# Four alternating attention layers as one list-scheduled pipeline of 128-token tiles, with block-diagonal scores

## The chip, the cores and the metric

The kernel runs on one core of one Trainium2 chip. The metric is the device time of one execution in microseconds (us), as the median over several runs. Engines are named as the profile does: PE is TensorE (matmul), PEld its weight loads, DVE is VectorE, ACT is ScalarE, POOL is GpSimd, SP the engine that issues the transfers. PSUM is the memory in which this kernel's matmuls leave their results, used here as eight banks; an eviction is the copy of a result out of it by ScalarE or VectorE. The clock in the tables is the share of its full clock that TensorE was granted, as the profile records it. A row group is a strip of 32 of TensorE's rows; in these kernels small matmuls are placed on different row groups so that they run side by side.

## The reference

One sequence of 2048 tokens, 512 features, 32 heads of 16. Four residual layers alternate: A is linear attention over the whole sequence, B is softmax attention over a sliding window of 256 keys. All in bfloat16.

```python
def _A_ref(x, wqkv, wo):                 # ... q, k, v: 32 heads of 16
    phi = lambda t: jnp.where(t > 0, t + 1, jnp.exp(t)) + 1e-6
    pq, pk = phi(q), phi(k)
    kv = jnp.einsum("bhsd,bhse->bhde", pk, v)
    z = jnp.einsum("bhsd->bhd", pk)
    num = jnp.einsum("bhqd,bhde->bhqe", pq, kv)
    den = jnp.einsum("bhqd,bhd->bhq", pq, z)[..., None] + 1e-6
    o = num / den
    # ... heads together
    return o @ wo
def _B_ref(x, wqkv, wo):                 # W = 256
    scores = jnp.einsum("bhqd,bhkd->bhqk", q, k) * (Dh ** -0.5)
    mask = (idx[:, None] - idx[None, :] >= 0) & (idx[:, None] - idx[None, :] < W)
    p = _softmax(jnp.where(mask[None, None], scores, -1e9), axis=-1)
    # ... p @ v, heads together
    return o @ wo
x = x + _A_ref(_layernorm(x), A_wqkv, A_wo)
x = x + _B_ref(_layernorm(x), B_wqkv, B_wo)
x = x + _A_ref(_layernorm(x), A_wqkv, A_wo)
x = x + _B_ref(_layernorm(x), B_wqkv, B_wo)
```

A needs the sum over all tokens (kv, z) before any of its outputs: a true barrier. B needs for a query only the 256 keys up to it.

## The kernel before

Each layer is a few phases, and every engine ends one phase before the next begins. B's attention phase goes pair of heads by pair of heads through a ring of three PSUM score buffers:

```python
def emit_scores(pe, pg):                      # two heads, 128 keys, up to 384 queries
    sl = pg % NSLOT                           # NSLOT = 3
    if pg >= NSLOT:
        pe.wait_ge(s_exp.h, s_exp.v(pg - NSLOT + 1))
    # ...
    for e in range(2):                        # two row groups of TensorE at once
        mm = pe.matmul(ST[sl][:, e, 0:n], lhsT, rhs, start=True, stop=True,
                       tile_position=(32 * (hs % 4), 0))
    s_st.inc(mm)
# TensorE's order
for pg in range(npairs):
    if pg + LA < npairs:                      # LA = 2
        emit_scores(pe, pg + LA)
    emit_pv(pe, pg)                           # waits for the masks of pg; 6 matmuls of 17 columns
# ScalarE
a.activation(self.PTs[:, j % NJS, hp[0] : hp[0] + 2, 0:n], ST[sl][:, :, 0:n],
             ACT.Exp, bias=self.zero1[:], scale=DH ** -0.5)
# VectorE: two triangular masks for each of the two heads
for e in range(2):
    op = v.tensor_tensor(self.PTs[:, js, hs, 0:P], self.PTs[:, js, hs, 0:P], self.maskHi[:], ALU.mult)
    if j + 2 < T:
        op = v.tensor_tensor(self.PTs[:, js, hs, 2 * P : 3 * P],
                             self.PTs[:, js, hs, 2 * P : 3 * P], self.maskLo[:], ALU.mult)
```

The softmax here doesn't subtract the row's maximum and nothing guards it: scores larger than these inputs give would overflow.

## Time and profile before

Median 845 us (843.5 to 846.3).

| stretch, us | what | TensorE | VectorE | ScalarE | clock |
|---|---|---|---|---|---|
| 193 to 402 | attention of the first B | 84% | 80% | 96% | 0.50 |
| 607 to 818 | attention of the second B | 84% | 79% | 95% | 0.50 |

The lines of the page for the whole span: totals of busy time, busy tenths in 40 slices with the granted TensorE clock, and the costliest groups of instructions (line, engine, operation, tiles, shapes and count, then busy us and mean ns of one, then idle time before it and what ended it).

```profile
span 840.9 us, 16707 instructions
PE 666.5 (79%) x5794; PEld 330.4 (39%) x5824; DVE 596.2 (71%) x2784; ACT 614.4 (73%) x856; POOL 6.5 (1%) x24
...
PE   0779685897888888888857877589888888888878
...
DVE  6669695437878778788767776943488787787865
ACT  1668234458999999999557763345599999999983
...
PEclk9989797996555555555779998979955555555559
...
L894 ACT ACTIVATE PTs<-st,zero_15 128x768 bf16<-128x768 f32 (+2 forms) x512 | 404.7, 860 | 21.7 <-PE st L849 10.3
L931 DVE TENSOR_TENSOR PTs<-PTs,maskHi 128x128 bf16<-128x128 bf16 x1024 | 219.5, 220 | 78.9 <-ACT PTs L894 78.1
L868 PE MATMUL U<-vB,PTs 128*128 128x17 bf16 x2880 | 163.0, 179 | 67.5 <-DVE PTs L935 62.9
L849 PE MATMUL st<-qT,kT 16*128 16x384 bf16 (+2 forms) x512 | 121.3, 472 | 2.2 <-PEq L320 2.2
```

Half of the span is B's attention: the long runs of 9 in ScalarE's row, over 5 in the clock's row. There TensorE and VectorE are some 80% busy, and TensorE's clock is half.

### The profile page before, as it was taken

To read this page: it belongs to the slowest core of one execution; us is meant where nothing else is said; L and a number is where in the kernel's file an instruction comes from. 1 tells how busy PE (TensorE), PEld (TensorE's weight loads), DVE (VectorE), ACT (ScalarE), POOL (GpSimd) and SP (SyncE) were. 2 spreads that over 40 slices of the span, in tenths; PEclk is the share of its full clock that TensorE was granted. 3 is DMA by queue.
4 is the path that set the end of the run, shared out by engine and by line. 5 is a ranking of instruction groups with operands and counts; after the bars stand their busy time and mean duration, and the time that the engine had idled before them with its cause. 6 is when DMAs were issued, how large, how long until landed. Compare 5 with 4: busy or idle time off the path is not lost. (4 is left out here: it accounts for less than half of the span.)

```text
span 840.9 us, 16707 instructions
## 1 busy us (share of the span) xinstructions
PE 666.5 (79%) x5794; PEld 330.4 (39%) x5824; DVE 596.2 (71%) x2784; ACT 614.4 (73%) x856; POOL 6.5 (1%) x24
## 2 busy tenths in 40 slices
PE   0779685897888888888857877589888888888878
PEld 0333542343343334433533344344333434334344
DVE  6669695437878778788767776943488787787865
ACT  1668234458999999999557763345599999999983
POOL 1000000000000000000000000000000000000000
PEclk9989797996555555555779998979955555555559
DMA  8000000000000000000000000000000000000003
GB/s 299 0 1 1 1 1 1 1 1 1 1 2 2 2 2 1 2 1 2 1 1 0 1 1 1 1 1 1 1 1 2 2 2 2 2 1 2 1 2 101
DMA packets 5971, 9.46 MB, mean 11 GB/s; under 512 B 384, under 2 KB 4992, under 8 KB 5888
## 3 DMA queue, kind: packets, MB, share of 16 engines
q1 hardware_dynamic: 5472, 6.29, 2.2%
q0 software_dynamic: 416, 2.10, 0.7%
q8 instruction: 47, 0.77, 0.4%
q14 instruction: 36, 0.29, 0.1%
HBM read 6.29 MB, written 2.10 MB: 10 GB/s over the span
## 5 line engine op out<-in xcount | busy, mean ns | idle before, releaser
L894 ACT ACTIVATE PTs<-st,zero_15 128x768 bf16<-128x768 f32 (+2 forms) x512 | 404.7, 860 | 21.7 <-PE st L849 10.3
L931 DVE TENSOR_TENSOR PTs<-PTs,maskHi 128x128 bf16<-128x128 bf16 x1024 | 219.5, 220 | 78.9 <-ACT PTs L894 78.1
L868 PE MATMUL U<-vB,PTs 128*128 128x17 bf16 x2880 | 163.0, 179 | 67.5 <-DVE PTs L935 62.9
L868 PEld LDWEIGHTS U<-vB,PTs 128*128 128x128 bf16 x2880 | 116.1, 106 | 244.5 <-DVE PTs L935 228.5
L935 DVE TENSOR_TENSOR PTs<-PTs,maskLo 128x128 bf16<-128x128 bf16 x896 | 194.8, 217 | 0.0
L849 PE MATMUL st<-qT,kT 16*128 16x384 bf16 (+2 forms) x512 | 121.3, 472 | 2.2 <-PEq L320 2.2
L849 PE MATMUL st<-qT,kTB 32*128 32x384 bf16 (+2 forms) x512 | 122.4, 473 | 0.0
L338 PE MATMUL pst<-ident,xn 128*128 128x128 bf16 x256 | 30.6, 276 | 71.2 <-DVE xn L436 66.4
L376 PE MATMUL pss<-xnT,wB_qk 128*128 128x512 bf16 x248 | 61.9, 390 | 0.6 <-issue 0.2
L376 PE MATMUL pss<-wA_qkv,xnT 128*128 128x512 bf16 x255 | 61.3, 383 | 0.1
L398 ACT ACTIVATE xnT<-pst 128x512 bf16<-128x512 bf16 x64 | 34.8, 595 | 31.7 <-PE pst L338 31.4
L470 DVE TENSOR_SCALAR kTB<-kT,maskB 128x512 bf16<-128x512 bf16 x32 | 11.3, 353 | 64.7 <-ACT kT L417 64.7
L251 ACT ACTIVATE tmpE<-pss,zero_15 128x512 f32<-128x512 f32 x64 | 44.1, 689 | 15.9 <-PE pss L376 8.0
L338 PEld LDWEIGHTS pst<-ident,xn 128*128 128x128 bf16 x256 | 20.2, 119 | 84.2 <-DVE xn L436 51.0
L671 ACT ACTIVATE oTtA<-pstA 128x512 bf16<-128x512 bf16 x32 | 19.1, 597 | 36.2 <-PE pstA L549 36.2
L911 DVE TENSOR_TENSOR o_tok<-U,densb 128x128 bf16<-128x128 f32 x128 | 37.3, 292 | 9.9 <-issue 0.4
L252 ACT ACTIVATE tmpR<-pss,zero_15 128x512 bf16<-128x512 f32 x64 | 44.0, 688 | 0.0
L255 DVE TENSOR_SCALAR tmpE<-tmpE 128x512 f32<-128x512 f32 x64 | 26.9, 420 | 23.7 <-ACT tmpR L252 23.7
L417 ACT ACTIVATE qT<-pss 128x512 bf16<-128x512 f32 x32 | 19.1, 597 | 32.7 <-PE pss L376 32.7
L436 DVE TENSOR_SCALAR xn<-xres,ln_mv,ln_rstd 128x512 bf16<-128x512 bf16 x64 | 26.1, 431 | 18.1 <-PE pst L338 7.3
L376 PEld LDWEIGHTS pss<-wA_qkv,xnT 128*128 128x128 bf16 x256 | 25.5, 100 | 32.5 <-issue 3.9
L376 PEld LDWEIGHTS pss<-xnT,wB_qk 128*128 128x128 bf16 x256 | 25.5, 101 | 30.4 <-issue 2.8
(84 smaller groups left out, 647.5 us busy)
## 6 DMA issues: line engine op xcount, KB each, us to landing
xres<-in_A_x_dram SPq DMA_DIRECT2D x4, 512.0 KB, 5.4
out_dram<-xres SPq DMA_DIRECT2D x16, 128.0 KB, 1.7
wA_qkv<-in_A_wqkv_dram SPq DMA_DIRECT2D x1, 1536.0 KB, 10.2
wB_nat<-in_B_wqkv_dram POOLq DMA_DIRECT2D x1, 1536.0 KB, 9.1
wA_o<-in_A_wo_dram SPq DMA_DIRECT2D x1, 512.0 KB, 11.8
wB_o<-in_B_wo_dram POOLq DMA_DIRECT2D x1, 512.0 KB, 9.6
```

Source lines behind the costliest of these rows:

```text
L251: a.activation(self.tmpE[:, js, :], ps_ap, ACT.Exp, bias=z)
L252: return a.activation(self.tmpR[:, js, :], ps_ap, ACT.Relu, bias=z)
L255: v.tensor_scalar(self.tmpE[:, js, :], self.tmpE[:, js, :], 1.0, 1e-6, op0=ALU.min, op1=ALU.add)
L338: mm = pe.transpose(pst[sl2][:, kt, :], self.xn[:, sl2, kt * P : (kt + 1) * P], self.ident[:])
L376: mm = pe.matmul(pss[:, sl, :], lhsT, rhs, start=(kt == 0), stop=(kt == 3))
L398: s_cp.inc(a.activation(self.xnT[:, :, t * P : (t + 1) * P], pst[sl2][:], ACT.Copy))
L849: mm = pe.matmul(ST[sl][:, e, 0:n], lhsT, rhs, start=True, stop=True, tile_position=(32 * (hs % 4), 0))
L868: mm = pe.matmul(ut[:, hs, 0:17], lhsT, rhs, start=(ci == 0), stop=(ci == len(cl) - 1))
L894: a.activation(self.PTs[:, j % NJS, hp[0] : hp[0] + 2, 0:n], ST[sl][:, :, 0:n], ACT.Exp, bias=self.zero1[:], scale=DH ** -0.5,)
L911: v.tensor_tensor(self.o_tok[:, jd, fd * P : (fd + 1) * P].rearrange("p (h d) -> p h d", d=DH), ut[:, :, 0:DH], dsb.to_broadcast([P, 8, DH ...
L931: op = v.tensor_tensor(self.PTs[:, js, hs, 0:P], self.PTs[:, js, hs, 0:P], self.maskHi[:], ALU.mult)
L935: op = v.tensor_tensor(self.PTs[:, js, hs, 2 * P : 3 * P], self.PTs[:, js, hs, 2 * P : 3 * P], self.maskLo[:], ALU.mult,)
```

## The change

The intent: make all layers one stream of 128-token tiles, so that the projections, norms and evictions of one tile run under the exps of another, and cut the work of the attention itself. The whole program is built as a graph of operations with priorities; a list scheduler in the kernel's Python file orders them on each engine, gives out the eight PSUM banks, and may place an eviction on ScalarE or VectorE. The core of the diff (the rest, nearly all of the file, is cut):

```diff
-for li, kind in enumerate(["A", "B", "A", "B"]):      # phase after phase
-    ...
+def build(self):
+    self.setup()
+    self.layer_a_keys(1, 0)      # first A: keys, values, queries of all tiles
+    self.barrier(1)              # kv sums, M = kv @ Wo, denominators
+    self.middle(2)               # tile by tile: A's output, B, the next A's keys and values
+    self.barrier(2)
+    self.middle(3)               # tile by tile: A's output, B, output
 # scores: two heads (block-diagonal keys) by 64 keys, 320 queries, four row groups at once
+for gq in range(4):
+    rows = slice(32 * gq, 32 * gq + 32)
+    m = e.matmul(K.ps(ps[gq])[:, 0:n], K.kB[rows, j % 4, 2 * f + b, :, :],
+                 K.XQ[rows, f, 64 * blk:64 * blk + n], ..., tile_position=(32 * gq, 0))
-    ACT.Exp, bias=self.zero1[:], scale=DH ** -0.5,
+    e.activation(K.pb[...], K.PS[:, b0:b1 + 1:b1 - b0, 0:n], ACT.Exp, bias=0.0, scale=0.25)
 # one mask instruction for four head pairs, both triangles
+    x = K.pb[:, sl, f, :, o:o + 320].rearrange("p g (w c) -> p g w c", c=64)[:, :, 0:5:4, :]
+    return e.tensor_tensor(x, x, K.tri[:]..., ALU.mult)
 # transposes of normalised tiles and of B's output: by the SP queue, most of them
+    return self.on("SP", name, lambda e: e.dma_start_transpose(out(), src()), ...)
 # 1/sqrt(var) on GpSimd, tile by tile, instead of Ln and Exp on ScalarE for all tiles
+    self.on("POOL", "pow", lambda e: e.tensor_tensor(K.rs[:, t, :], K.ve[:, t, :], K.negh[:], ALU.pow), ...)
+PAR = dict(cap_s=6, cap_d=2, ...)   # PSUM banks for scores, and for all else, in the middle phases
```

## The prediction

> **What bounds the kernel now.** It runs in phases; windows over the stages show two limits.
> - The two sliding-attention phases (193 to 402 and 607 to 818 us) take 420 of 841 us. ScalarE is busy 200 of 209 us in each: 256 exps follow each other every 0.84 us (timeline). The granted TensorE clock is 0.50 there. VectorE (166 of 209) masks in 1920 small multiplies of 220 ns, one every 0.135 us: about 259 us in all.
> - The other 421 us (both linear layers, B's projections, output products) are bound by no engine: ScalarE and VectorE are 44 to 73% busy. Each phase drains before the next.
>
> **What the change does.**
> 1. *Exp.* A diagonal block took 384 queries per 128 keys, now 320 per 64 keys of two heads: 344k to about 290k ScalarE columns. The 512 exps stay 512, at 640 columns. Their bias becomes an immediate. The Trainium skill ("ScalarE: Activation LUTs", What ACT_TABLE_LOAD costs) puts a pointer operand at about 93 ns; the trace agrees: a 512-wide exp with pointer bias takes 689 ns, a copy 597. Estimate: 0.84 becomes 0.62 us per exp; 430 becomes about 300 us. The relu (64 x 688 ns) goes too.
> 2. *Masks.* 1920 multiplies become 256 over four head pairs: about 259 to 95 us.
> 3. *TensorE.* Scores: four row tiles at once instead of two. Value products stay 2880, at 34 columns instead of 17. Weight products M = KV.Wo replace num, and half the transposes go to the DMA queue (69).
> 4. *Order.* Three long phases (A keys; A out + B + next A keys; A out + B) instead of eight; projections, norms and evictions run under the exps.
>
> **Engine sums after**, counted from the built instruction order, costed at start-to-start times of the trace: ScalarE 300 (exp) + 32 (phi) + 43 (88 copies) = 375 us. VectorE about 390 us. TensorE at full clock (512 columns: 0.216 us, as in the trace): projections 230, value products 80, scores 33, rest 30, = 373, plus some 590 changes of tiling at an estimated 0.08 us = 47: 420 us. Nearly balanced.
>
> **Time.** A-keys prologue 60; barrier and fill of three tiles 18; 16 tiles of middle phase at 13.5 = 216; barrier 22; 16 tiles at 12.2 = 195; tail 9: 520 us. The tile times allow 15 to 20% over the busiest engine, because the evictions share two PSUM banks and scores six. About 130 us of the gain is exps, the rest overlap.
>
> **Clock.** The skill ("TensorE: Matmul & The Clock Gate", HAM clock gate) has two states, half and full, by activity; the trace shows 0.50 in attention, 1.00 in dense projections. With projections mixed in I expect 0.9.
>
> **What would show it.** Right: exp group near 725 ns each, ScalarE total near 375, mask group below 110 us, clock above 0.85, no engine idle over 15 us except at two barriers; ScalarE busy above 80% in the middle phases. Wrong: clock near 0.5 to 0.7 in the middle phases (PE bound, +60 us or more); long ScalarE waits on TensorE scores (PSUM coupling); waits on DMA transposes, whose cost no line of this trace shows.
>
> **What would make it wrong.** Half clock; fewer stalls in the static order than allowed (470); transposes slow or in the way.
>
> Predicted 518 us, 8 in 10 between 470 and 570; faster 0.98, same 0.01, slower 0.01.

## The result, and the profile after

The changed kernel takes 534.2 us (532.6 to 536.3, 4 runs); it is correct. The ratio to before is 0.632 (95% interval 0.631 to 0.634).

The same parts of the page after the change:

```profile
span 532.9 us, 16311 instructions
PE 445.8 (84%) x7124; PEld 289.6 (54%) x7124; DVE 415.8 (78%) x988; ACT 389.4 (73%) x673; POOL 59.1 (11%) x114
...
PE   0399987888999999999877997888998989787676
...
DVE  4497769788988899999765759899799889777543
ACT  0166762689988889899886343389799889899962
POOL 8860001001000010000000000100000000000000
PEclk9999999989999999999887999899899999999756
...
L624 ACT ACTIVATE pb<-ps 128x640 bf16<-128x640 f32 (+4 forms) x512 | 305.9, 675 | 33.1 <-PE ps L612 30.2
L632 DVE TENSOR_TENSOR pb<-pb,tri 128x512 bf16<-128x512 bf16 x224 | 92.7, 415 | 16.4 <-ACT pb L624 15.0
L612 PE MATMUL ps<-XQ,kB 32*128 32x320 bf16 (+4 forms) x1024 | 80.7, 305 | 26.5 <-ACT pb L624 24.9
L652 PE MATMUL ps<-vB,pb 128*128 128x34 bf16 x2880 | 90.6, 179 | 4.9 <-DVE xres L565 2.0
```

The table of stretches, as the windows view gives it for the phases of the new kernel (start:end, length, then busy us and count of each engine, granted clock, DMA share, GB/s), and one stretch of steady state:

```profile
0.00:22.00 22.00, 0.44 (x4) 0.35 (x4) 7.79 (x31) 1.28 (x1) 18.45 (x44) 1.00 0.88 286
22.00:77.00 55.00, 53.18 (x574) 35.53 (x572) 42.55 (x103) 36.31 (x63) 13.69 (x23) 1.00 0.01 2
77.00:98.70 21.70, 16.07 (x248) 10.95 (x248) 18.18 (x36) 6.90 (x15) 2.19 (x4) 1.00 0.01 2
98.70:297.00 198.30, 179.06 (x2868) 108.67 (x2864) 166.07 (x411) 170.22 (x297) 14.86 (x27) 0.96 0.17 29
297.00:346.00 49.00, 42.05 (x667) 32.87 (x667) 37.59 (x81) 17.82 (x33) 2.91 (x6) 0.97 0.02 4
346.00:525.00 179.00, 151.82 (x2740) 99.84 (x2738) 142.01 (x326) 156.32 (x266) 6.97 (x12) 0.92 0.14 32
...
180.00:230.00 50.00, 47.78 (x785) 29.54 (x784) 46.03 (x112) 45.29 (x76) 4.39 (x8) 1.00 0.17 34
```

In the stretch of steady state TensorE, VectorE and ScalarE are 96, 92 and 91% busy at once. Over the whole first middle phase they are 90, 84 and 86% busy, over the second 85, 79 and 87%. The exps fill these two phases of 198 and 179 us. Around them stand 22 us in which little but GpSimd works, 55 us of the first A's keys, values and queries, 22 us to fill the pipeline after the first barrier, and 49 us at the second barrier, in which ScalarE is busy for 18.

The attention itself became cheaper for TensorE. Two pieces of the timeline (start, length, engine, line, operation and count) show it. The first is from the old order, in the run `before_both` below, where TensorE hardly waits; the second is from the changed kernel:

```profile
301.33 0.50 PE L850 MATMUL st<-qT,kT 16*128 16x384 bf16 x2
301.76 0.33 PE L869 MATMUL U<-vB,PTs 128*128 128x17 bf16 x6
302.02 0.50 PE L850 MATMUL st<-qT,kTB 32*128 32x384 bf16 x2
302.45 0.33 PE L869 MATMUL U<-vB,PTs 128*128 128x17 bf16 x6
```

```profile
201.74 0.76 PE L652 MATMUL ps<-vB,pb 128*128 128x34 bf16 x24
202.43 0.32 PE L612 MATMUL ps<-XQ,kB 32*128 32x320 bf16 x4
202.68 0.77 PE L652 MATMUL ps<-vB,pb 128*128 128x34 bf16 x24
203.29 1.02 PE L438 MATMUL ps<-wA,XQ 128*128 128x512 bf16 x4
```

After: 0.25 us from start to start for the scores of eight heads by 64 keys, and 0.61 us for 24 value products, or 0.69 us when scores come next, 0.08 us more. Two score groups and 24 value products serve eight heads by 128 keys: 2 x (0.25 + 0.08) + 0.61 = 1.27 us, so an estimate is 0.32 us for a pair of heads by 128 keys. In the old order a pair takes 0.69 us (from 301.33 to 302.02, or 301.76 to 302.45) at the half clock.

### The profile page after: what moved, and what is told of

Same layout as the page of the kernel before. It is cut to its first block, busy times and chain, and to the rows that moved or that the text cites. A ratio compares the mean times of both kernels' runs of the same rounds, so it can differ in the third digit from the quotient of the medians.

```text
span 532.9 us, 16311 instructions
## 1 busy us (share of the span) xinstructions
PE 445.8 (84%) x7124; PEld 289.6 (54%) x7124; DVE 415.8 (78%) x988; ACT 389.4 (73%) x673; POOL 59.1 (11%) x114
## 4 chain that ended last, share of the span: by engine, by line
PE 45%; DVE 30%; ACT 14%; DMA 5%; POOL 4%; issue 2%; POOLq 0%; DVEq 0%
PE ps L438 14%; ACT pb L624 10%; PE ps L452 10%; PE ps L652 9%; DVE xres L565 5%; PE ps L612 5%; DVE pb L632 4%; PE ps L592 3%; DVE vB L427 3%; DVE kB L579 3%; DVE stats L399 3%; DMA oT<-o 3%; DMA XQ<-xn 2%; DVE pqd L559 2%; DVE XQ L463 2%
## 5 line engine op out<-in xcount | busy, mean ns | idle before, releaser
L624 ACT ACTIVATE pb<-ps 128x640 bf16<-128x640 f32 (+4 forms) x512 | 305.9, 675 | 33.1 <-PE ps L612 30.2
L632 DVE TENSOR_TENSOR pb<-pb,tri 128x512 bf16<-128x512 bf16 x224 | 92.7, 415 | 16.4 <-ACT pb L624 15.0
L612 PE MATMUL ps<-XQ,kB 32*128 32x320 bf16 (+4 forms) x1024 | 80.7, 305 | 26.5 <-ACT pb L624 24.9
L652 PE MATMUL ps<-vB,pb 128*128 128x34 bf16 x2880 | 90.6, 179 | 4.9 <-DVE xres L565 2.0
L652 PEld LDWEIGHTS ps<-vB,pb 128*128 128x128 bf16 x2880 | 80.8, 97 | 18.8 <-DVE xres L565 3.9
L452 PE MATMUL ps<-xT,wBp 128*128 128x128 bf16 x1024 | 69.5, 221 | 3.0 <-DVE kB L579 0.9
L438 PE MATMUL ps<-wA,XQ 128*128 128x512 bf16 x256 | 67.0, 395 | 4.4 <-DMA XQ<-xn 2.8
L452 PEld LDWEIGHTS ps<-xT,wBp 128*128 128x128 bf16 x1024 | 58.3, 98 | 12.2 <-DVE kB L579 1.2
L565 DVE TENSOR_TENSOR xres<-ps,xres 128x512 bf16<-128x512 f32 x64 | 43.8, 686 | 12.3 <-PE ps L438 11.8
L399 DVE BATCH_NORM_STATS2 stats<-xres 128x6 f32<-128x512 bf16 x64 | 43.1, 683 | 3.3 <-DMA xres<-in_A_x_dram 3.1
```

Of the source, the lines that this page charges most:

```text
L399: self.on("DVE", "stats", lambda e: e.bn_stats(K.stats[:, t, :], K.xres[:, t, :]), key, dve(512), rd=[("xres", t)], wr=[("stats", t)])
L438: m = e.matmul(K.ps(ps), lhs(c), rhs(c), start=c == 0, stop=c == 3)
L452: m = e.matmul(K.ps(ps)[:, f * P:(f + 1) * P], w(c, f), xT(c), start=c == 0, stop=c == 3)
L565: self.on("DVE", "res", lambda e: e.tensor_tensor(K.xres[:, t, :], K.ps(po), K.xres[:, t, :], ALU.add), key, dve(512), rd=[("xres", t)], w ...
L612: m = e.matmul(K.ps(ps[gq])[:, 0:n], K.kB[rows, j % 4, 2 * f + b, :, :], K.XQ[rows, f, 64 * blk:64 * blk + n], start=True, stop=True, tile ...
L624: return e.activation(K.pb[:, sl, f, g0:g1 + 1, o:o + n], K.PS[:, b0:b1 + 1:b1 - b0, 0:n], ACT.Exp, bias=0.0, scale=0.25)
```

## The experiments

Twelve kernels ran, all correct, each beside the kernel before on the same chip. The first four ask what really bounded the attention phase before; the other eight ask what carries the new kernel.

| run | median, us | ratio to before |
|---|---|---|
| changed kernel | 534.2 | 0.632 |
| before_imm | 830.9 | 0.983 |
| before_mask | 812.6 | 0.961 |
| before_both | 783.7 | 0.927 |
| before_warm | 920.2 | 1.089 |
| ptr_bias | 550.0 | 0.651 |
| fast_start | 525.3 | 0.622 |
| banks44 | 693.7 | 0.822 |
| pe_transpose | 561.6 | 0.665 |
| blk128 | 588.5 | 0.696 |
| two_te | 541.1 | 0.641 |
| build_order | 1382.3 | 1.638 |
| tuned | 515.4 | 0.611 |

### before_imm, before_mask, before_both: two edits of the change, in the old order

```diff
 # before_imm
-                            bias=self.zero1[:],
+                            bias=0.0,
 # before_mask: four multiplies of a head pair as one
-                    for e in range(2):
-                        ...
+                    x = self.PTs[:, js, h0 : h0 + 2, :].rearrange("p h (w c) -> p h w c", c=P)[:, :, 0 : 2 * nw - 1 : 2, :]
+                    op = v.tensor_tensor(x, x, self.maskHL[:, 0:nw, :].unsqueeze(1).to_broadcast([P, 2, nw, P]), ALU.mult)
```

> The kernel before, with only the bias of the 512 attention exps turned from a pointer into an immediate. Theory (ScalarE bounds the attention phases): 512 x 0.093 us = 48 us less, so 797 us (790 to 805). Rival (TensorE at its half clock, or the VectorE masks, bound them just as much, since both are over 80% busy there): less than 15 us gained, 830 us or more.

> The kernel before, with the four mask multiplies of a pair of heads merged into one, 1920 to 512 instructions, about 259 to 170 us of VectorE. Theory (ScalarE bounds): within 1% of before. Rival (the masks are part of the bound): over 20 us faster.

> Both edits in the kernel before. Theory: with the exps at 0.75 us the masks may begin to matter, 0 to 15 us below the immediate-bias run alone. Rival (masks bound): over 20 us below it.

Measured: 14 us gained by the immediate bias, 33 by the merged masks, 61 by both. The exp did get as much shorter as expected (811 ns instead of 900), but only 14 of the expected 48 us came off the time. The theory that ScalarE bounds that phase falls; the rivals' ranges held in all three runs (14 us is under 15, 33 over 20, and both edits came 47 below the immediate bias alone). But no single other engine is shown as the bound either: the gains of the two edits do not add up (14 + 33 = 47, not 61). The stretch from 220 to 380 us of before, before_imm, before_mask and before_both, in this order (busy us of PE, PEld, DVE, ACT with their counts; clock near the end):

```profile
220.00:380.00 160.00, 135.99 (x1474) 63.71 (x1472) 127.01 (x821) 152.64 (x194) 0.00 (x0) 0.50 0.01 2
```

```profile
220.00:380.00 160.00, 138.34 (x1515) 65.39 (x1514) 129.40 (x844) 143.14 (x199) 0.00 (x0) 0.50 0.01 2
```

```profile
220.00:380.00 160.00, 151.74 (x1599) 69.14 (x1595) 101.97 (x313) 158.77 (x210) 0.00 (x0) 0.50 0.01 2
```

```profile
220.00:380.00 160.00, 153.89 (x1701) 74.51 (x1701) 107.24 (x333) 152.50 (x222) 0.00 (x0) 0.50 0.01 2
```

With the immediate alone, ScalarE falls to 89% busy and just waits. With the masks alone, ScalarE rises to 99%, and full exps start every 0.784 us (seven in a row took 5.71 us, the last one some 1.01): there ScalarE has no room left, which fits that the immediate bias then gives 29 us and not 14. With both, TensorE at its half clock is 96% busy, ScalarE 95%, and an exp (edges counted in) comes every 160 / 222 = 0.72 us instead of 160 / 194 = 0.82.

What fits is a round trip. In the code shown above, TensorE takes the scores of pair p + 3 only after the value products of pair p, which wait for p's masks, which wait for p's exp. One turn of that circle yields three pairs. Its recorded steps in the kernel before are 0.90 us (exp), 0.62 (four masks), 0.33 (values) and 0.50 (scores): 2.35 us, or 0.78 us a pair, and 0.82 was measured; the rest is 0.12 us a turn for four hand-overs. The high busy shares came from a circle in which every engine's record covers much of the turn. By this estimate a step that gets shorter counts by a third: 512 x 0.089 / 3 = 15 us for the bias and 512 x 0.20 / 3 = 34 us for the masks (0.62 to 0.42 us), and 14 and 33 were measured; for both it gives 49, and 61 were measured, so it is not the whole account. It is an estimate that fits the single edits; no run changed the number of score buffers, so it is argued, not shown. Shown is that neither ScalarE nor VectorE alone was the bound.

### before_warm: keep TensorE busier to raise its clock

```diff
                 n = nqb(j) * P
                 mm = None
+                pe.matmul(ST[sl][:, 0, 0:n], self.wB_o[:, 0, 0:P], self.xnT[:, 0, 0:n], start=True, stop=True)
```

> The kernel before, with one more dense matmul (128 rows, up to 384 columns, its result overwritten at once by the scores) for each of the 512 score pairs, to keep TensorE active. Theory (the half clock costs nothing because ScalarE bounds): granted clock in attention rises from 0.50 to over 0.8 and the time stays within 2% of before. Rival (the half clock is part of the bound): over 20 us faster at the higher clock.

This run failed as a test. The time rose by 75 us, and the clock did not rise; the same stretch as above:

```profile
220.00:380.00 160.00, 159.89 (x1433) 58.86 (x1429) 111.01 (x695) 140.08 (x165) 0.00 (x0) 0.50 0.01 2
```

TensorE's records cover 159.89 of 160 us, and the granted clock stays at 0.50. So the run says nothing on what a full clock would have been worth in the old order. It does say that TensorE had little room: 0.42 us more of dense matmul (start to start) for a pair cost 75 / 512 = 0.15 us each. And it shows that one dense matmul mixed into every pair does not raise the clock.

### ptr_bias: give ScalarE its 48 us back, in the new order

```diff
-                    return e.activation(K.pb[...], K.PS[...], ACT.Exp, bias=0.0, scale=0.25)
+                    return e.activation(K.pb[...], K.PS[...], ACT.Exp, bias=K.zb[:], scale=0.25)
```

> The changed kernel, same order, with a pointer bias for its 512 attention exps again: 48 us more ScalarE work. Theory (three engines nearly balanced, ScalarE over 88% busy in the two middle phases): 25 to 48 us slower than the changed kernel, 559 to 582 us. Rival (TensorE, the busiest, bounds and ScalarE has room): less than 12 us slower, under 546 us.

Measured: 15.7 us slower, between the theory's 25 and the rival's 12. Both were too sharp: ScalarE's work counts by a third. In the two traces TensorE, VectorE and ScalarE run their instructions in the same order, so nothing but the exps' length differs on them. ScalarE's waits for scores shrink (busy us, mean ns, and idle before; the changed kernel's line stands above with 33.1 us idle, 30.2 of it for scores):

```profile
L625 ACT ACTIVATE pb<-ps,zb 128x640 bf16<-128x640 f32 (+4 forms) x512 | 343.1, 774 | 14.7 <-PE ps L613 14.2
```

The full exp of 640 columns alone went from 709 to 810 ns. The Trainium skill ("ScalarE: Activation LUTs", What ACT_TABLE_LOAD costs) gives 186 ns + 0.833 ns a column with an immediate and about 280 with a pointer, 719 and 813 ns here; the traces agree.

### blk128 and its control two_te: the old block shape in the new order

```diff
-        blk = 2 * j + b                       # two heads by 64 keys, block-diagonal
-        n = min(320, S - 64 * blk)
+        n = min(384, S - P * j)               # one head by 128 keys
 # ... keys, masks (128x128 triangles), values and the exps' buffer to match
 # two_te, and part of blk128 (to fit the memory): two tE buffers instead of three
```

> The changed kernel with the score blocks of before: one head by 128 keys by 384 queries, no block diagonal, masks of 128x128; the same number of exps, masks, score and value matmuls, in the same list schedule (two buffers for the linear layers' exps instead of three, to fit the memory). ScalarE gets 61,440 more columns, 51 us, and VectorE's masks twice the columns, about 60 us. Theory (three engines nearly balanced, so work on either ScalarE or VectorE makes it the bound): 30 to 65 us slower than the changed kernel, 564 to 599 us. Rival (TensorE alone bounds): under 549 us.

> Control for blk128: the changed kernel with two instead of three buffers for the linear layers' exps. Within 1% of the changed kernel, 529 to 540 us; if not, the difference is taken off what blk128 shows.

The control missed its range by 1 us: 541.1, or 7 us above the changed kernel. Against the control the old block shape costs 588.5 - 541.1 = 47 us (the two orders differ also, as said under pe_transpose), inside the range of the theory and outside the rival's. In its steady state VectorE is now the busiest (48.71 of 50 us) and TensorE has fallen to 44.13:

```profile
200.00:250.00 50.00, 44.13 (x644) 24.92 (x642) 48.71 (x102) 47.51 (x69) 5.06 (x7) 1.00 0.17 31
```

So the block-diagonal shape does pay. It saves work of both ScalarE (768 to 640 columns an exp) and VectorE (1024 to 512 columns a mask instruction, 683 to 415 ns); how much of the 47 us belongs to each, and how much to the lower mean clock (0.91 against 0.945 in the control), the run does not tell. For TensorE the shape matters little: in the trace of blk128 a group of four 384-column score matmuls takes 0.27 us to the next group, and 24 value products 0.68 us before scores, so by the same sum about 0.33 us for a pair.

### build_order: the same instructions without the list schedule's order

```diff
+        both = {o.i: len(o.engs) > 1 for o in self.g.ops}
+        for o in self.g.ops:
+            o.engs = {o.eng: o.engs[o.eng]}      # engines as the first schedule chose them
+        order = schedule(self.g, self.par, inorder=True)
 # in schedule(): an engine may only take the next of its operations in the order of building
+                if inorder and todo[e][0] != i:
+                    back.append((k, i))
+                    continue
```

> The changed kernel's instructions on the same engines, but each engine takes them in the order in which the program builds them (tile by tile: front of tile j+3, scores and values of j, output of j), in place of the list schedule's. Theory (the order, not the operations, gives most of the overlap): the dependent steps of a front, about 8 us a tile, and of an output, about 5 us, are exposed, so over 700 us. Rival (any order of one pipeline would do): under 600 us.

Measured: 1382 us, 2.6 times the changed kernel and 1.6 times the old one, with the same operations on the same engines. The theory stands, and the size was beyond its floor. ScalarE waits for TensorE in long single waits (the waits view: us in total, times, longest):

```profile
ACT tE L467 <- PE ps L444: 245.1, 32, 13.9
ACT pb L630 <- PE ps L618: 239.7, 47, 21.0
ACT vB L433 <- PE ps L598: 170.0, 22, 20.8
```

TensorE itself waits for the queue's transposes, 309 us in all (130.5, 97.5 and 81.4 for `xT`, `oT` and `XQ`; under 6 us in the changed kernel). The page's line for the first:

```profile
L458 PE MATMUL ps<-xT,wBp 128*128 128x128 bf16 x1024 | 113.8, 311 | 136.0 <-DMA xT<-xn 130.5
```

TensorE is 48% busy, and its clock averages 0.62 instead of 0.95, so its 446 busy us became 664: the emptier order also had the lower clock. The operations of the new kernel, taken tile by tile in this plain order, lose to the old kernel. A good order is the gain's condition; only this one plain order was tried.

### banks44: PSUM banks divided 4 and 4

```diff
-    cap_s=6, cap_d=2, cap_e=6, ...
+    cap_s=4, cap_d=4, cap_e=6, ...
```

> The changed kernel with its PSUM banks divided 4 for scores and 4 for the rest, in place of 6 and 2. Theory (two banks for the rest are not the limit, score banks feed ScalarE): the next score group waits for both exps of the last one, ScalarE idles some 0.3 us for each of 256 groups, 30 to 75 us slower. Rival (the two banks for evictions are the limit): over 10 us faster.

The direction was right and the size far off: 159 us slower, not 30 to 75. With four banks the scores of the next group wait for both exps of the last, and ScalarE's wait for scores grows from 30.2 us in the changed kernel to:

```profile
ACT pb L624 <- PE ps L612: 136.5, 204, 3.1
```

That is 106 us more of waiting. TensorE idles more, its clock falls from 0.95 to 0.81 and its busy time rises from 446 to 501 us; neither was in the expectation, and whether the idling lowered the clock is not shown (in before_warm the clock was 0.50 without idling). Two more banks for the evictions are not worth two banks of the scores. What two banks cost the evictions no run shows alone; in the two middle phases of the changed kernel the waits view has TensorE wait 25 us for exps that free score banks, and under 3 us for any other one cause.

### pe_transpose: no transposes by the queue

```diff
-        if not by_pe:
+        if False:
             return self.on("SP", name, lambda e: e.dma_start_transpose(out(), src()), ...)
```

> The changed kernel with all 69 queue transposes done by TensorE: about 16 us more TensorE work and about 35 us more evictions on ScalarE or VectorE. Theory (all three balanced): 20 to 40 us slower. Rival (the queue's transposes, 2.5 us each to landing, hold up the pipeline): no slower, or faster.

Measured: 27 us slower, inside the theory's range. TensorE is busy 26 us more (16 were expected), VectorE and ScalarE 31 together:

```profile
PE 471.5 (84%) x7400; PEld 305.0 (54%) x7400; DVE 430.7 (77%) x1035; ACT 405.1 (72%) x695; POOL 60.0 (11%) x114
```

The 69 transposes by the queue, which land after 2.4 to 2.5 us each, are well hidden and save three engines work.

One reservation holds for this run, banks44 and blk128: the list schedule was drawn up anew for each, with priorities that were not fitted to it, and the traces of pe_transpose and banks44 show other orders on TensorE, VectorE and ScalarE. How much of a difference is the order's was not tested. One buffer less moved the time by 7 us (two_te), and priorities alone by 10 (tuned).

### fast_start: the first inverse square roots not behind the constants

In the changed kernel the first tile is normalised at 21 us. The timeline shows why: GpSimd makes constants that are needed only after the first barrier, and the inverse square roots stand behind them in its order.

```profile
18.43 1.97 POOL L391 MEMSET pb<- 128x1024 bf16 x2
20.48 3.85 POOL L402 TENSOR_TENSOR rs<-ve,negh 128x1 f32<-128x1 f32 x6
21.09 0.41 DVE L403 TENSOR_SCALAR xn<-xres,mv,rs 128x512 bf16<-128x512 bf16 x1 [6.02 <-POOL rs L402]
21.56 1.24 PE L415 MATMUL ps<-ident,xn 128*128 128x128 bf16 x8 [21.56 <-DVE xn L403]
```

```diff
-            return self.on("POOL", name, emit, key, (ns, ns + 60), **kw)
+            return self.on("POOL", name, emit, key + 120 if key > 0 else key, (ns, ns + 60), **kw)
 # ... and the same for the VectorE steps of these constants
```

> The changed kernel with lower priority for the GpSimd setup constants, so that the first inverse square roots don't queue behind 16 us of them. Theory: the first normalised tile comes at about 7 us instead of 21, limited then by the weights' landing at about 9 us; 10 to 14 us faster, 520 to 524 us. Rival (loads or the later pipeline take the time back): less than 4 us gained.

Measured: 525.3 us, 9 us gained, just short of the range. TensorE's first transpose now starts 14 us earlier:

```profile
7.25 1.24 PE L415 MATMUL ps<-ident,xn 128*128 128x128 bf16 x8 [7.25 <-DVE xn L403]
```

The other 5 us are lost again on the way to the barrier; where exactly was not settled.

### tuned: a faster version

```diff
-k_pv=0.669, k_wo=0.738, k_next=1.117, k_q=2.69, k_ao=4.2, k_kv=2.62, k_v=0.435, ... pe_first=4, pe_last=1
+k_pv=0.667, k_wo=0.758, k_next=1.094, k_q=2.18, k_ao=4.2, k_kv=0.77, k_v=0.218, ... pe_first=2, pe_last=3
 # on top of fast_start
```

> An attempt at a faster version: fast_start with priorities moved (B's q and k later, values earlier in key, three last tiles and two first transposed by TensorE). The two barriers and the middle phases keep their work, so small: 0 to 10 us faster than fast_start, 515 to 525 us. If the schedule's own assumptions are off by more than that, as slow or slower.

Measured: 515.4 us (513.8 to 517.0), ratio to before 0.611: 10 us below fast_start and 19 below the changed kernel. These priorities were found by a random search over the kernel's own list schedule. It is the fastest of all the versions.

## Why the prediction was right or wrong, point by point

**The time.** 534 us against 518, inside the range of 470 to 570. The sum was right partly by luck, because its errors cancel:

| term | predicted | measured | how read |
|---|---|---|---|
| prologue (keys of the first A) | 60 | 77 | start to 77.0 |
| barrier and fill | 18 | 22 | to the first exp, 98.7 |
| first middle phase | 216 | 198 | to 297 |
| second barrier | 22 | 49 | to the next exp, 346 |
| second middle phase | 195 | 179 | to the last exp, 525 |
| tail | 9 | 8 | to the end, 533 |
| sum | 520 | 533 | |

**The prologue** was mis-sized because the start was overlooked: 21.6 us pass before TensorE's first transpose, behind GpSimd's constants. "No engine idle over 15 us except at two barriers" was wrong there. fast_start shows that the order of GpSimd was the cause of that start, and that 9 us of it were on the critical path.

**The second barrier** was mis-sized by 27 us. Part of this is where the line is drawn: the table cuts at exps, and TensorE is busy for 42 of the 49 us, also with the last tiles' outputs and the first of the next phase. Phase and barrier together were 247 us against 238. The chain of waits goes through the 16 kv sums, one after the other on TensorE from 310.6 to 315.9 us, with VectorE and ScalarE waiting 4.8 and 5.9 us for what follows, and through the queries' feature maps: 240 of the 256 matmuls of the second A's query projections, 15 tiles of 16, stand in these 49 us, because the program gives them a priority after the sums. The program holds these sums back because they need two PSUM banks of their own. That is read from the trace and the code; no run changed it.

**The middle phases** were over-sized. Engine sums were about right: ScalarE 389 us instead of 375, VectorE 416 instead of 390, TensorE 446 instead of 420. But I allowed 15 to 20% over the busiest engine for waits on PSUM. The first phase took 11% more than TensorE was busy (198.3 us for 179.1), the second 15% more than ScalarE (179.0 for 156.3). A tile takes 198 / 16 = 12.4 us, not 13.5. That the "evictions share two PSUM banks" costs this slack is not borne out: banks44 gave them two more, at the expense of scores, and lost 159 us.

**"Nearly balanced"** held. Extra work on ScalarE alone counts by a third (ptr_bias), on ScalarE and VectorE together nearly in full (blk128, 47 us for 51 and 60), on all three partly (pe_transpose, 27 us).

**The bound of the kernel before** was the step that failed. I read ScalarE's 200 of 209 us and the spacing of 0.84 us as "ScalarE bounds attention", and so put "about 130 us of the gain" on the exps. before_imm took 89 ns off each of 512 exps and gained 14 us, not 48; before_mask, on the engine that I had set aside, gained more, 33. That masks, exps and TensorE's half-clock matmuls were steps of one turn, so that shortening one helped in part, is the account that fits (see before_imm); it was not tested. The exps did shorten as predicted (the full one takes 709 ns against some 725 foretold; four in a row took 2.49 us, so (2.49 - 0.71) / 3 = 0.59 us from start to start, against 0.62), but what part of the 311 us is theirs cannot be given as one number: the gains were not additive in the one pair that was tried.

**The clock** came out as expected, 0.95 against 0.9, but not for a reason that is shown, so that is luck. The prediction put it to "projections mixed in", and before_warm mixed a dense matmul into every pair and stayed at 0.50. What raised the clock is open. At half clock a pair of heads cost TensorE 0.69 us, and now 0.32. The block shape has little part in this (0.33 in blk128); four row groups instead of two, and the full clock, are not told apart by any run.

**Masks**: 102 us (92.7 + 9.2) against 95 and a limit of 110. **ScalarE** was to be over 80% busy in the middle phases, and is 86 and 87%. **Transposes by the queue** were feared as unknown; in pe_transpose the kernel without them was 27 us slower.

## What to carry to other kernels

A high busy share beside two other high ones, in a loop with few buffers, is not yet a bound: shorten one step and see whether the time follows, before a large gain is put on it. Operations that balance three engines need an order that keeps all three fed: here the same operations in a plain order were 2.6 times slower. In a static schedule look at the least watched engine too: constants at the head of GpSimd's order held up TensorE's first work by 14 us, and 9 us of it came off the time.

## What the Trainium skill lacked or had wrong

- "TensorE: Matmul & The Clock Gate", The HAM clock gate: it says that the ratio follows how busy TensorE has been recently. What counts as busy is missing, but for a remark on transposes. In before_warm TensorE's records cover 159.89 of 160 us and the granted clock is 0.50; in the changed kernel 47.78 of 50 us, and it is 1.00.
- "ScalarE: Activation LUTs", What ACT_TABLE_LOAD costs: its durations held (709 and 810 ns against 719 and 813). Its overlap of 93 ns for back-to-back instructions did not: in before_mask exps recorded at 1006 ns started every 0.784 us (seven in 5.71 us), 0.22 us of overlap, so a recorded duration can be longer than what the engine needs.
- "TensorEngine Tiling (Array Packing)", Key Properties: a change of tiling mode drains TensorE, it says, with no figure. Here 24 value products took 0.69 us up to a group of score matmuls on four row groups and 0.61 up to dense matmuls: 0.08 us for that change. The four 320-column score matmuls took 0.25 us to the next group's start; 320 columns at the 2.4 GHz of "TensorE: Matmul & The Clock Gate" are 0.13, so an estimate is 0.12 us for the change back.
- "DMA: Bandwidth & Descriptors", DMA Transpose: no latency for one transpose within SBUF. 128x512 bfloat16 landed after 2.4 to 2.5 us (69 of them).
- No page that I read gives GpSimd's power function: 561 ns for 128x1 in the changed kernel's profile, whose spans on GpSimd are rough.
